# A gated linear-attention block and its MLP on one core: another sequence of turns, and the state's part of y on 128 by 64 tiles in place of 64 by 64

## The chip, the cores and the metric

The kernel runs on one core of one Trainium2 chip. The metric is the device time of one execution in microseconds (us), lower being better. Before the change the median of three executions is 481.49 us (481.31 to 482.73). The profile comes from the execution of 481.31 us; its span, from the first to the last recorded instruction, is 479.3 us.

## The reference

Two stages follow each other. The first is a gated recurrence for each of 4 batches and 8 heads, over 768 tokens with a head size of 48; the second is a LayerNorm and a two-layer MLP (384 to 1536 to 384) with a residual.

```python
def _attn_ref(q, k, v, alpha):                 # all (4, 8, 768, 48), fp32
    state = np.zeros((B, H, D, D))
    for t in range(S):
        state = alpha[:, :, t, :, None] * state + np.einsum('bhd,bhe->bhde', k[:, :, t], v[:, :, t])
        y[:, :, t] = np.einsum('bhd,bhde->bhe', q[:, :, t], state)
    return y

def _moe_ref(x, g_ln, w_ch1, w_ch2):           # x: (4, 768, 384), the heads side by side
    xn = (x - mu) / np.sqrt(var + 1e-06) * g_ln
    ch = np.maximum(xn @ w_ch1, 0.0) @ w_ch2
    return x + ch
```

The weights arrive as 64-bit floats and are rounded to fp32 on the chip.

## The kernel before

The tokens are cut into 6 chunks of 128, so there are 24 attention blocks (chunk c, batch b). One block is a Python generator with 22 steps. Each step issues a few instructions and then yields. These are the steps that matter here:

```python
    def attention(c, b):
        ...
        nc.gpsimd.tensor_mul(qk[:, 1, :, :D], raws.pop(("k", c, b)), ek)      # GpSimd: k scaled
        yield
        nc.vector.tensor_mul(qk[:, 0, :, :D], raws.pop(("q", c, b)), eq)      # VectorE: q scaled
        ...
        # TensorE: 8 transposes into qkT [112, 2, 4, 128]: head 2p in rows 0..47, head 2p+1 in rows 64..111
        for p in range(NP):                                                   # NP = 4 pairs of heads
            for i in range(2):
                rows = slice(64 * i, 64 * i + D)
                nc.tensor.matmul(aps[i][:, p], qkT[rows, 1, p], qkT[rows, 0, p], start=True, stop=True)
        yield
        for i in range(2):                                                    # VectorE: causal mask
            nc.vector.copy_predicated(out=at[:, i], data=aps[i], mask=...)
        ...
        yps = [ps.tile([P, NP, D], FP32, name=f"yps{i}", tag=("s", "a")[i], bufs=(2, 3)[i]) for i in range(2)]
        sides = [slice(64 * s, 64 * s + 64) for s in range(2)]                # the two halves of the tokens
        if c > 0:                                                             # y, part of the carried state (line 284)
            for p in range(NP):
                for i in range(2):
                    rows = slice(64 * i, 64 * i + D)
                    for s in sides:
                        nc.tensor.matmul(yps[i][s, p], qkT[rows, 0, p, s], sts[b][rows, p, i],
                                         start=(p == 0), stop=False)
        for p in range(NP):                                                   # y, part within the chunk (line 289)
            for i in range(2):
                for s in sides:
                    nc.tensor.matmul(yps[i][s, p], at[:, i, p, s], vt[:, 2 * p + i],
                                     start=(c == 0), stop=(c == 0 or p == NP - 1))
        yield
        for i in range(2):                                                    # ScalarE: y out of PSUM (line 294)
            nc.scalar.copy(out=x.rearrange("p (a b d) -> p a b d", b=2, d=D)[:, :, i], in_=yps[i])
        yield
        ...                        # sps: k'v of the chunk (line 302); st: added to the state (307), gated on GpSimd (312)
        nc.vector.bn_stats(stats, x); nc.vector.bn_aggr(mv, stats)            # LayerNorm
        ...
        nc.vector.tensor_scalar(out=xn, in0=x, scalar1=mv[:, 0:1], scalar2=rstd,   # line 323
                                op0=AOP.subtract, op1=AOP.mult)
        yield
        ...
        for f in range(NF):                                                   # TensorE: transposes of xn (line 330)
            nc.tensor.transpose(xps[:, f], xn[:, f * P:(f + 1) * P], ident)
```

`sts[b]` holds the state of a pair of heads in 112 rows and 96 columns, as two blocks of 48 by 48 on the diagonal; the rest is zero.

Other generators run beside the blocks. The MLP of chunk 0 is made of plain products (lines 342 and 354). The MLP of the later chunks uses fast matrix products of 15 and 7 multiplications (lines 515 and 409), whose sums are made ahead on GpSimd (for the weights) and on VectorE (for the activations):

```python
    def combine_first():           # sums of the first layer's weights, 17 turns of two GpSimd instructions (line 467)
        for n, op, out, x, y in (...):
            for i in range(2):
                op(out[i], x[i], y[i])         # 128x384, then 128x128
            yield
    def sums():                    # letter S
        yield from combine_first()
        yield from combine_weights()           # second layer's weights, GpSimd (line 374)
```

Every engine works through its own instructions in the order in which they were issued, and that order is set by one string. Each letter lets one generator run to its next yield:

```python
    turns = {chr(ord("a") + n): attention(n // B, n % B) for n in range(NCB * B)}       # a..x: the blocks
    turns |= {chr(ord("A") + i): take_weights(i) for i in range(len(pieces))}           # A..L: round a piece of the weights
    turns |= {"M": mlp(), "S": sums(), "R": relus(), "X": ..., "N": ...}                # X, N: sums of activations on VectorE
    with tc.manual_schedule():
        for turn in ORDER:
            next(turns[turn], None)
```

Of the kernel before, what the change touches and what calls it, by code (L numbers as in the profile page):

```python
# [9 lines left out]
FP32 = mybir.dt.float32  # L10
# [11 lines left out]


ORDER = (
    "abaacbababadacbbdaacaacadbcbbbaacdadbAbbccBbdcAbCcddbddeccfcbaBfefeahfafeagdhdfb"
    "dfcbeAaefdhcBbdedgBeedfcdecfebgicbagefcdhfCgefeigghefiahfeiggdcCdhegCEcggdcFjfAM"
    "jFegMDEjMjhhfMMffFMMMDiMegElMDhhDMhhMlFMkgiGIGihEGgHIhMHMMeMkIMIMMikMMjlGMiHHLgL"
    "JjfKMJejehMKfMJgMMKLhhKMMhMMghMhiMkiMfSSijjgSijkhglMjgXXjXkSSliSXSSMMjSlinXSkMkX"
    "XMSXjSiSXMMSkMlMSMkMSmXMSMMMMijlMMMMMXMMRlMkMMiMklMMRMmmmMiMlkRkljMnMSRnmMSjMMMM"
    "MknlMMRMMliljkmMnnMMMSRMpiMMMMmMkpmlMMkRMRoMMmMkMmRMlpoMoMNMRlNniMMNnkMSMMnNmMMm"  # L30
    "kMjMMRpMmnnlRpjolMMNkNMMMMooNMlnMMMMjlMNXjXMXnqXXMXXmXMmnXmMqpMoMMMnoMMMMmMMoqMX"
    "MoMMXqMmMMMopqorRMMopMMpMpqMmMronnoMMMMMrRMMRnsrMpMMMqpMMRppMorpmMqRqMrqMMRMoMpM"
    "tMRnMtMMMpMorMsMRrMMtMqMRsNMNtmRMMrmRMNoMoMnMqstMMMLnMMMpJrqsMMRpNnrpqMMsMNMNtMr"
    "NoqoMppMMMMMuNsXMMXXuXXXMMXsqrXvXMuMsMMMXMMMqMqXMMrqrrrtMuMMMMMtMrMMsMsuMMsMvMvR"
    "qrsMMMMRRMMusMtMtMMMuRsMMvMvMMMMtsuRMvrMMswMMMRtMuqswMMtMRsRqMMRMutMxNsttMRMvMtM"
    "NwMvRNMMNuMMurstvvMtMstRMMMxMMMMNrwNtNxMxMwMMuvMxNMMMvMtMXMXMXXvwMXvXuXXMMwuMMXw"
    "XwMMMMvMMMxMMMMMMMMMMMxXxwMMMxxuMMMMwMwxwRwMMMMMMMMxMMuxMMMMMRxRuMMxwxwMMMuMMRxR"
    "RMRMMMMRvvMuMMRNMNRwwNMuMMvMuxRxRvMMMMMNxwMMvMMxMwMNvNMvMxMwNMNwMMMMXXXXMXMXXMMX"
    "MMMXMXMMMMMMMMMMMMRMMMMMMXMMMMMRRMMMMMMMMMMMRRMMMMMRMMMMMMMMRMRMMMMMRMRMMNMMMNNM"
    "MMNMMMMMMMRMRMMMNMNMNNMMMMMMMMMM"  # L40
)


# [1 line left out]
def kernel(  # L45
# [8 lines left out]
    w_ch2: bass.AP,  # L54
    out: bass.AP,
):

# [22 lines left out]
    nc = tc.nc  # L83

    B, S, H, D = q.shape
    DM = H * D
    DF = w_ch1.shape[1]
    P = 128
    NCB = S // P
    NP = H // 2  # L90
    R = 64 + D
# [11 lines left out]
    ps = ctx.enter_context(tc.tile_pool(name="ps", bufs=2, space=bass.MemoryType.PSUM))  # L103
# [100 lines left out]
    sts = [cpool.tile([P, NP, 2, D], FP32, name=f"st{b}") for b in range(B)]  # L204
# [17 lines left out]
    def attention(c, b):  # L222
# [25 lines left out]
        qkT = work.tile([R, 2, NP, P], FP32, name="qkT", tag="qkT", bufs=2)  # L248
# [11 lines left out]
        at = ats[b % len(ats)]  # L260
        aps = [ps.tile([P, NP, P], FP32, name=f"aps{i}", tag="a", bufs=3) for i in range(2)]
# [3 lines that stand above are left out]
                nc.tensor.matmul(aps[i][:, p], qkT[rows, 1, p], qkT[rows, 0, p],  # L265
                                 start=True, stop=True)
# [7 lines left out]
                nc.sync.dma_start(gate, row.rearrange("o a c -> c (o a)"))  # L274
        yield
        vt = raws.pop(("v", c, b))
        yps = [ps.tile([P, NP, D], FP32, name=f"yps{i}", tag=("s", "a")[i], bufs=(2, 3)[i]) for i in range(2)]
        sides = [slice(64 * s, 64 * s + 64) for s in range(2)]
        if c > 0:
            for p in range(NP):  # L280
                for i in range(2):
                    rows = slice(64 * i, 64 * i + D)
                    for s in sides:
                        nc.tensor.matmul(yps[i][s, p], qkT[rows, 0, p, s], sts[b][rows, p, i],  # L284
                                         start=(p == 0), stop=False)
        for p in range(NP):
            for i in range(2):
                for s in sides:
                    nc.tensor.matmul(yps[i][s, p], at[:, i, p, s], vt[:, 2 * p + i],  # L289
                                     start=(c == 0), stop=(c == 0 or p == NP - 1))  # L290
        yield
        x_of[c, b] = x = work.tile([P, DM], FP32, name="x", tag="x", bufs=9)
        for i in range(2):
            nc.scalar.copy(out=x.rearrange("p (a b d) -> p a b d", b=2, d=D)[:, :, i],
                           in_=yps[i])
        yield
        if c + 1 < NCB:
            sps = ps.tile([R, NP, D], FP32, name="sps", tag="s")
# [294 lines left out]
    def sums():  # L593
# [4 lines left out]
        yield from combine_weights()  # L598

    turns = {chr(ord("a") + n): attention(n // B, n % B) for n in range(NCB * B)}  # L600
    turns |= {chr(ord("A") + i): take_weights(i) for i in range(len(pieces))}
    turns |= {"M": mlp(), "S": sums(), "R": relus(),
# [35 lines left out]
```

## Time and profile before

| | busy us | share of the span | instructions |
|---|---|---|---|
| TensorE matmul (PE) | 463.2 | 97% | 4032 |
| TensorE weight load (PEld) | 387.4 | 81% | 4032 |
| VectorE (DVE) | 328.5 | 69% | 571 |
| GpSimd (POOL) | 203.2 | 42% | 203 |
| ScalarE (ACT) | 152.5 | 32% | 349 |

A matmul on fp32 data is recorded as two instructions, each with its own weight load; a transpose is one. Records of matmuls overlap, because they are pipelined: the mean of 383 ns of a matmul of 256 columns is no pitch. How fast matmuls follow each other is read from the chain of waits, where 12 instructions of line 409 take 1.95 us, or from the starts of two instructions that follow each other. The span of 40 slices gives 12 us to a slice. In it the matmul engine is busy nine tenths or more of every slice but the first two, the tenth (108 to 120 us) and the last. The bytes moved are 33.9 MB, most of them in the first 84 us.

### The profile page before, as it was taken

The numbers are of one execution on the slowest core, as the hardware profiler recorded it, in microseconds if no ns is written. First come the engines' busy times: TensorE is split into PE (matmuls) and PEld (weight loads), VectorE is DVE, ScalarE is ACT, GpSimd is POOL, SyncE is SP. The second block draws the span as 40 slices with busy tenths as digits, with TensorE's granted clock in tenths as the row PEclk, the third lists the DMA queues.
The fourth block names the chain that finished last, engine by engine and source line by source line (L and its number), as shares of the span: only waits on it lengthen the run. The fifth ranks groups of instructions, "written<-read, shape, count | busy, mean of one in ns | idle before, by whom it ended". The sixth has DMA issues, their size and how long they took to land.

```text
span 479.3 us, 9886 instructions
## 1 busy us (share of the span) xinstructions
PE 463.2 (97%) x4032; PEld 387.4 (81%) x4032; DVE 328.5 (69%) x571; ACT 152.5 (32%) x349; POOL 203.2 (42%) x203
## 2 busy tenths in 40 slices
PE   5799999997999999999999999999999999999997
PEld 2668555554688899998889998889998889987996
DVE  3799899825577688748677567678565666665732
ACT  5567444501033442133351222542103152123300
POOL 5134200093479984107474217472414282145611
PEclk9999999998999999999999999999999999999999
DMA  8977466102031300232200413110010000000000
GB/s 269 335 207 218 142 197 191 42 23 60 18 84 37 98 18 12 72 101 64 72 18 0 133 51 85 34 34 1 34 36 0 2 1 18 16 34 0 2 33 34
DMA packets 32501, 33.89 MB, mean 71 GB/s; under 512 B 13108, under 2 KB 28596, under 8 KB 32456
## 3 DMA queue, kind: packets, MB, share of 16 engines
q1 hardware_dynamic: 31912, 33.12, 22.8%
q8 instruction: 32, 0.52, 0.4%
q10 hardware_dynamic: 544, 0.13, 0.1%
q14 instruction: 13, 0.11, 0.1%
HBM read 28.49 MB, written 4.76 MB: 69 GB/s over the span
## 4 chain that ended last, share of the span: by engine, by line
PE 93%; DVE 5%; ACT 1%; DMA 1%; issue 1%; DVEq 0%
PE ops L409 29%; PE hps L515 28%; PE hps L342 7%; PE ops L354 6%; PE aps L265 5%; PE yps L289 5%; PE tps L252 4%; PE lps L229 3%; PE yps L284 3%; PE sps L302 2%; PE xps L330 2%; DVE at L269 1%; DVE xn L323 1%; DMA ra<-in_alpha_dram 1%; DVE w L166 1%
## 5 line engine op out<-in xcount | busy, mean ns | idle before, releaser
L515 PE MATMUL hps<-sum,w 128*128 128x256 f32 x200 | 52.1, 383 | 0.0
L567 ACT ACTIVATE hT<-hT 128x512 f32<-128x512 f32 x60 | 36.5, 629 | 24.2 <-POOL hT L537 12.2
L409 PE MATMUL ops<-w,sum 128*128 128x192 f32 x240 | 42.6, 327 | 0.0
L409 PE MATMUL ops<-w,hT 128*128 128x192 f32 x240 | 42.5, 327 | 0.0
L409 PE MATMUL ops<-ws,hT 128*128 128x192 f32 x240 | 42.3, 326 | 0.0
L515 PEld LDWEIGHTS hps<-sum,w 128*128 128x128 f32 x200 | 36.7, 190 | 5.3
L269 DVE COPY_PREDICATED at<-consts,aps 128x512 f32<-128x512 int32 x48 | 32.1, 722 | 12.9 <-PE aps L265 12.8
L312 POOL TENSOR_TENSOR st<-st,gate 128x384 f32<-128x384 f32 x20 | 20.1, 1005 | 48.9 <-PE hps L342 23.4
L236 POOL TENSOR_TENSOR qk<-rk,ek 128x384 f32<-128x384 f32 x24 | 26.1, 1092 | 32.8 <-ACT ek L233 26.1
L409 PEld LDWEIGHTS ops<-w,sum 128*128 128x128 f32 x240 | 39.3, 190 | 0.5
L409 PEld LDWEIGHTS ops<-ws,hT 128*128 128x128 f32 x240 | 39.4, 190 | 0.3
L409 PEld LDWEIGHTS ops<-w,hT 128*128 128x128 f32 x240 | 39.2, 190 | 0.4
L427 POOL TENSOR_TENSOR ob<-u,x 128x192 f32<-128x192 f32 x10 | 7.1, 712 | 71.9 <-issue 38.5
L534 POOL TENSOR_TENSOR hT<-hT,u 128x512 f32<-128x512 f32 x10 | 13.2, 1315 | 50.3 <-DVE u L533 50.2
L354 PE MATMUL ops<-w,hT 128*128 128x384 f32 x96 | 33.5, 502 | 0.0
L342 PE MATMUL hps<-xT,w 128*128 128x512 f32 x72 | 32.4, 597 | 0.0
L252 PEld LDWEIGHTS tps<-consts,qk 128*112 128x112 f32 x192 | 22.8, 137 | 11.2 <-issue 4.0
L252 PE MATMUL tps<-consts,qk 128*112 128x128 f32 x192 | 29.8, 281 | 2.1 <-DVE at L269 1.0
L515 PE MATMUL hps<-xT,w 128*128 128x256 f32 x120 | 31.0, 381 | 0.0
L265 PEld LDWEIGHTS aps<-qkT 48*128 48x128 f32 x384 | 24.0, 187 | 7.4 <-issue 4.5
L289 PE MATMUL yps<-rv,at 128*64 128x48 f32 x768 | 27.5, 224 | 1.9 <-DVE at L269 1.4
L265 PE MATMUL aps<-qkT 48*128 48x128 f32 x384 | 28.7, 285 | 0.7 <-ACT qkT L256 0.7
(127 smaller groups left out, 939.1 us busy)
## 6 DMA issues: line engine op xcount, KB each, us to landing
ws<-in_moe_w_ch_dram SPq DMA_DIRECT2D x12, 768.0 KB
ra<-in_alpha_dram SPq DMA_DIRECT2D x24, 192.0 KB
rk<-in_k_dram SPq DMA_DIRECT2D x24, 192.0 KB
rq<-in_q_dram SPq DMA_DIRECT2D x24, 192.0 KB
rv<-in_v_dram SPq DMA_DIRECT2D x24, 192.0 KB
out_dram<-ob SPq DMA_DIRECT2D x24, 192.0 KB
row<-eq SPq DMA_DIRECT2D x20, 2.0 KB
gate<-row SPq DMA_DIRECT2D x20, 2.0 KB
```

What stands on the lines that cost most here:

```text
L229: nc.tensor.matmul(lps[:, :DM], tri, la, start=True, stop=True)
L236: nc.gpsimd.tensor_mul(qk[:, 1, :, :D], raws.pop(("k", c, b)), ek)
L252: nc.tensor.transpose(tps[:, p], qks[b][:, i, p].rearrange("p a b -> p (a b)")[:, :R], ident)
L265: nc.tensor.matmul(aps[i][:, p], qkT[rows, 1, p], qkT[rows, 0, p], start=True, stop=True)
L269: nc.vector.copy_predicated(out=at[:, i], data=aps[i], mask=mask.unsqueeze(1).broadcast_to([P, NP, P]))
L289: nc.tensor.matmul(yps[i][s, p], at[:, i, p, s], vt[:, 2 * p + i], start=(c == 0), stop=(c == 0 or p == NP - 1))
L312: nc.gpsimd.tensor_mul(st, st, gate.unsqueeze(2).broadcast_to([P, NP, 2 * D]))
L342: nc.tensor.matmul(hps, w1[:, f, j * P:(j + 1) * P], xT_of[c][:, f], start=(f == 0), stop=(f == NF - 1))
L354: nc.tensor.matmul(ops_of[b], hT_of[c][:, j, b], w2[:, j], start=(j == 0), stop=(j == NJ - 1))
L409: nc.tensor.matmul(acc, quarters(c, b)[0][n][:, j], win["b"][n][:, j], start=(j == 0), stop=(j == HJ - 1))
L515: nc.tensor.matmul(acc[:, i], w, b, start=True, stop=True)
L567: nc.scalar.activation(out=x, in_=x, func=AFT.Relu)
```

## The change

The change has two parts. In the first, the state's part of y is computed for a pair of heads at once. Before, each of the two heads had its own rows (48 of 64) and each half of the tokens its own columns, so that four tiles of 64 by 64 of the array were in use, with 48 columns of output each. Now both heads go through together: the 112 rows of `qkT` against the state's 112 rows and 96 columns, the two zero blocks included, on two tiles of 128 rows and 64 columns. That makes 8 matmuls of 96 columns for a block in place of 16 of 48. They stand between those of the chunk's own part, pair by pair. y now lies in one PSUM bank (tag `s`) instead of two (`s` and `a`), and ScalarE copies it out with one instruction instead of two.

The second part is the string. The sequence of turns is another one on all engines, [...]. Each block has the same 22 steps as before, and all other instructions and buffers are the same.

```diff
@@ the sequence of turns (16 lines; the parts that the prediction speaks of) @@
-    "abaacbababadacbbdaacaacadbcbbbaacdadbAbbccBbdcAbCcddbddeccfcbaBfefeahfafeagdhdfb"
-    "dfcbeAaefdhcBbdedgBeedfcdecfebgicbagefcdhfCgefeigghefiahfeiggdcCdhegCEcggdcFjfAM"
-    "jFegMDEjMjhhfMMffFMMMDiMegElMDhhDMhhMlFMkgiGIGihEGgHIhMHMMeMkIMIMMikMMjlGMiHHLgL"
-    "JjfKMJejehMKfMJgMMKLhhKMMhMMghMhiMkiMfSSijjgSijkhglMjgXXjXkSSliSXSSMMjSlinXSkMkX"
-    "XMSXjSiSXMMSkMlMSMkMSmXMSMMMMijlMMMMMXMMRlMkMMiMklMMRMmmmMiMlkRkljMnMSRnmMSjMMMM"
-    "MknlMMRMMliljkmMnnMMMSRMpiMMMMmMkpmlMMkRMRoMMmMkMmRMlpoMoMNMRlNniMMNnkMSMMnNmMMm"
-    "kMjMMRpMmnnlRpjolMMNkNMMMMooNMlnMMMMjlMNXjXMXnqXXMXXmXMmnXmMqpMoMMMnoMMMMmMMoqMX"
-    ... (9 lines cut)
+    "ababdaacbaabccaabacdacbaabadcbbbdcdAabbbdaBcCccdabAeddbcbdcffcdfeegacfcbagdhfbde"
+    "adbceBeegAdhfBCfdeabdfefcAheiBeafdeagjgbecfebcfcgeegfdefdgcghhihfdcgdegCCigMhMgD"
+    "DhMjEMEjFMhiDkhfMgfighFheMFFfMMIMEIhIDMgEjhMGhMgjMhgfMGiHMMGGkMMMMHeiJMkMlHJMigM"
+    "IMLJilHljMejKKjiLKeLjMhhfjSigSMhMlSMglSlhgiffMKkMhMhSSSMSSSMXiXkikXSXiimjMXXXSSM"
+    "MXkMMSkjMMXkMkMMSMMjMmMMjXkmMSlmiMSMMiMkMMXkMjMMMlMlmRMmMMMokSjlMlMnlMnMljnkMMMR"
+    "MjnMMMMSMMmMnMMmnRMMRRMoRSkiMlpklniMkpnjmMMRMmMRpkMRMNMMNmMlMiRkmMMiNMMnloMpRMSM"
+    "njNMMkplMoRMMMkMMNmjNMMlMMNNmonnMljomqMMlqMMlnXMMXMXmXnXXMXqMMMXmmXMMooMMMMpMpMn"
+    ... (9 lines cut)
@@ -274,25 +273,21 @@
                 nc.sync.dma_start(gate, row.rearrange("o a c -> c (o a)"))
         yield
         vt = raws.pop(("v", c, b))
-        yps = [ps.tile([P, NP, D], FP32, name=f"yps{i}", tag=("s", "a")[i], bufs=(2, 3)[i]) for i in range(2)]
+        yps = ps.tile([P, NP, 2, D], FP32, name="yps", tag="s")
         sides = [slice(64 * s, 64 * s + 64) for s in range(2)]
-        if c > 0:
-            for p in range(NP):
-                for i in range(2):
-                    rows = slice(64 * i, 64 * i + D)
-                    for s in sides:
-                        nc.tensor.matmul(yps[i][s, p], qkT[rows, 0, p, s], sts[b][rows, p, i],
-                                         start=(p == 0), stop=False)
         for p in range(NP):
+            if c > 0:
+                for s in sides:
+                    nc.tensor.matmul(yps[s, p].rearrange("p a b -> p (a b)"), qkT[:, 0, p, s],
+                                     sts[b][:R, p].rearrange("p a b -> p (a b)"),
+                                     start=True, stop=False)
             for i in range(2):
                 for s in sides:
-                    nc.tensor.matmul(yps[i][s, p], at[:, i, p, s], vt[:, 2 * p + i],
-                                     start=(c == 0), stop=(c == 0 or p == NP - 1))
+                    nc.tensor.matmul(yps[s, p, i], at[:, i, p, s], vt[:, 2 * p + i],
+                                     start=(c == 0), stop=(c == 0 or i == 1))
         yield
         x_of[c, b] = x = work.tile([P, DM], FP32, name="x", tag="x", bufs=9)
-        for i in range(2):
-            nc.scalar.copy(out=x.rearrange("p (a b d) -> p a b d", b=2, d=D)[:, :, i],
-                           in_=yps[i])
+        nc.scalar.copy(out=x, in_=yps.rearrange("p a b d -> p (a b d)"))
         yield
         if c + 1 < NCB:
             sps = ps.tile([R, NP, D], FP32, name="sps", tag="s")
```

The first letters S stand in the fourth line of both strings: in `MfSSijjgS` before and in `hhfjSigSMh` after. There `f`, `g` and `h` are the blocks (1, 1), (1, 2) and (1, 3).

## The prediction

> **What bounds the kernel now.** I read the shares first, then the slices, then the matmul engine's waits, then the chain of waits around the one place that stood out. The shares and slices of the page:
>
> ```profile
> PE 463.2 (97%) x4032; PEld 387.4 (81%) x4032; DVE 328.5 (69%) x571; ACT 152.5 (32%) x349; POOL 203.2 (42%) x203
> ...
> PE   5799999997999999999999999999999999999997
> ...
> PEclk9999999998999999999999999999999999999999
> ```
>
> TensorE is the bound, and it is short of work in the first two slices, in the tenth (108 to 120 us, where the granted clock also drops) and at the end. Its waits, longest first (us in total, times, longest):
>
> ```profile
> PE lps L229 <- ACT la L226: 4.3, 1, 4.3
> PE xps L330 <- DVE xn L323: 3.1, 1, 3.1
> PE yps L289 <- DVE at L269: 1.4, 2, 1.1
> ...
> PE hps L515 <- DVE hT L558: 0.8, 1, 0.8
> ```
>
> The first is the start (first data). The second is the only long wait in the steady part. The chain of waits there (start, length, what):
>
> ```profile
> 107.45 4.29 DVE xn L323
> 111.74 0.14 issue
> 111.87 0.87 PE xps L330 x3
> 112.75 3.65 PE ops L354 x8
> ...
> 124.71 0.61 PE yps L284 x32
> 125.32 1.07 PE yps L289 x32
> 126.39 2.78 PE ops L354 x8
> 129.17 0.44 PE tps L252 x4
> 129.60 2.58 PE ops L354 x8
> ```
>
> One LayerNorm subtraction takes 4.29 us. The list of the tile xn shows that this is an exception, and GpSimd's order of time shows what ran meanwhile:
>
> ```profile
> L323 DVE TENSOR_SCALAR xn<-x,mv,rstd x24: 461/476/4364, 33.9 to 407.4; 128x384 f32<-128x384 f32 x24
> ...
> 107.38 4.13 POOL L467 TENSOR_TENSOR w<-w 128x384 f32<-128x384 f32 x6
> 126.94 1.11 POOL L467 TENSOR_TENSOR rq<-w 128x384 f32<-128x384 f32 x1 [15.43 <-DVE qk L238]
> ```
>
> The median is 476 ns; this one began with a row of six GpSimd sums and ended 0.2 us after the last, when GpSimd ran out of work. When TensorE resumed, eight instructions of line 354 took 3.65 us, not the 2.58 us of a quiet place.
>
> To split the span I take from the trace the pitch of each kind of matmul instruction (start to start, same kind): 429 ns for 512 columns, 323 for 384, 216 for 256, 163 for 192, 109 for 128 (transposes); 61 for line 265, 29.2 for line 289, 28 for line 302 and 14.9 for line 284. A change of tile shape adds to this: 93 ns going into tiles (line 515 to 265: 309 for 216), 122 from line 289 or 302 and 141 from line 265 on leaving, 134 from line 284 to 289. Counts times pitches give 437.0 us, and the 121 changes of shape 14.2 us, together 451.2. The first matmul starts at 4.3 us and the end after the last start is 3.6 us. The other 20.3 us are excess: 11.5 before 48 us (waits and slow matmuls of the start), 4.8 from 108 to 120 us, 1.0 near 436 us, 3 spread out.
>
> [...] this one did not get in between six GpSimd instructions in a row, while others, at 158.1 and 187.7 us, got in between two. [...] 93 to 141 ns for a change, and 14.9 ns a step on four tiles against 29.2 on two. [...] After the 3.6 us between two matmul starts, the next ones of line 354 are 640 ns apart for some 1.5 us, not 323. A wait of 3.1 us thus cost 4.8.
>
> **The change part by part.**
>
> *State's part of y.* It removes 16 matmuls in each of the 20 blocks with c > 0, 320 in all: 640 instructions at 14.9 ns, 9.5 us. It adds 160 of 96 columns. No row has this shape, so I estimate it. Two tiles of 128 by 64 take 58.4 ns for two instructions of 48 columns; in the full array a column costs 0.835 ns ((429 − 109)/384), so 48 more columns add 40 ns. That is 98 ns for each matmul (two instructions on alternating tiles), 15.7 us in all. If the weight load came to be hidden, only 96 columns × 0.835 = 80 ns would be left, 12.8 us. So +6.1 us, at best +3.3.
>
> *Changes of shape.* State and chunk parts now share a shape, so 20 changes at 134 ns go, 2.7 us. The new sequence also has other neighbours: on TensorE I count 88 changes after for 121 before. At the costs above, 10.1 us for 14.2: −4.1 us.
>
> Sum on TensorE, which is the path: 6.1 − 4.1 = **+2.1 us** before rounding (453.3 for 451.2), −0.8 at best.
>
> *Copy of y.* Two copies of 326 ns become one of 384 columns, estimated at the 475 ns of the xT copy (same size, also from PSUM): 24 × (652 − 475) = 4 us less of ScalarE, which is 32% busy. Worth nothing directly. The tag `a` of three PSUM buffers loses one user, which may ease the start.
>
> *The sequence at 108 us.* Before, the subtraction of block (1, 3) stood on VectorE behind two sums that wait for TensorE (line 359), and so came when GpSimd was deep in its row of weight sums. After, (1, 1) and (1, 2) are placed around the first S, (1, 3) after the fourth, and the row of six S turns (`SSSMSSS`) comes behind all three. GpSimd instructions which wait for another engine (line 236) stand between S turns 2 and 3 and again after turn 4; at such places the subtractions got in before. I expect 4.8 us to shrink to 0.3. But GpSimd runs ahead freely: counting from the end of (1, 3)'s state sum, it reaches the second of these places after 0.9 + 4 × 1.45 + 1.0 = 7.7 us, and VectorE reaches (1, 3)'s subtraction after two line-354 groups, two sums and one product, 2 × 2.6 + 2 × 0.56 + 0.6 = 6.9 us. That is close. One chance in four that it misses, and then it waits some 7 us, of which I charge 6 to TensorE. Expected: −4.5 + 1.5 = **−3.0 us**.
>
> *The start.* VectorE was nearly full from 24 to 96 us before (11.6 of 12 us in most stretches), with the weight rounding. Ahead of the MLP's first product there are now 6 rounding steps of about 2.4 us on VectorE, before there were 8; the total up to the last weight piece is the same within 1 us (82.8 and 83.7). TensorE can thus start the MLP a little sooner, but the later pieces still hold it: I take **−1 us**, −3 to +2.5.
>
> Sum: 479.3 + 2.1 − 3.0 − 1.0 = 477.4 us of span. The metric is 2.2 us above the span (481.49 and 479.3): 479.6, which I round down to 479.0, because the row may also end a little faster than charged.
>
> **Rivals.** (1) *The sequence changes nothing, as VectorE's exclusion comes back elsewhere.* For it: all 24 subtractions still run beside GpSimd's work, and VectorE's sums with two SBUF inputs are stretched as well (1.1 us for 0.4 at 133 us). Against it: from 120 to 432 us all of that cost TensorE only some 2 us, since it has work queued. It would give 481 + 2 = 483.5. (2) *TensorE's work decides.* With a dearer state part, say 120 ns, the sum is +5.6 and the time about 482.5; with the cheap 80 ns it is 476. (3) *The start becomes the bound*, a weight piece arriving later than its product: the tightest place before was the fourth piece, whose rounding ended 4 us of VectorE work beyond TensorE's own; after, the tightest is 2.7 us. It speaks for a gain: 476.5. (4) *The row catches two subtractions and VectorE stands still for 12 us or more*: 487 and worse.
>
> **Range and chances.** The terms vary by about 2 (state part), 3 (the wait at 108) and 2.5 us (start), together some 4.5 us to each side: 474.5 to 484.5 us. 2% is 9.6 us, so faster would need under 471.9, all terms at their best and more, and slower over 491.1, a new stall of over 10 us. The work of all engines is the same within 1%, which leaves 0.95 for within 2%.
>
> **What would show it.** In the profile after: PE instructions 3712 (4032 − 640 + 320); the state group with about 49 ns of pitch an instruction, and with its neighbours some 1.7 to 1.75 us a block, as now (0.61 + 1.07); no subtraction on line 318 (the old 323) over 2.5 us before 130 us, and PE nines in the tenth slice with the clock at 9. If the state group shows 40 or 60 ns, the estimate of the fixed part was wrong. If a subtraction of 4 us or more stands in the chain again, the reading of GpSimd's row was wrong. If TensorE has more than 14 us of excess before 48 us, or less than 9, the start was. Wrong altogether would be a wait that the lists do not show me: for a PSUM buffer of tag `s`, which now alone holds y until it is copied out, or at the end, where the fast products of chunk 5 stand alone.

## The result, and the profile after

The changed kernel takes **475.15 us** (median; 473.87 to 475.65), the kernel before 481.71 us on the same chip (481.31 to 482.73): a ratio of 0.9857, 95% interval 0.9832 to 0.9882. The forecast of 479.0 had the direction right, and the time lies in the range (474.5 to 484.5), near its lower edge; but the gain is 6.6 us where 2.5 were forecast. The profiled span went from 479.3 to 471.8 us, by 7.5; this is what is accounted for below. It is 0.9 us more than the gain in the medians, because the profiled execution of the kernel after is its fastest, 1.3 us under its median, and that of before lies 0.4 us under its own.

The page of the kernel after, shares and slices:

```profile
PE 459.0 (97%) x3712; PEld 388.5 (82%) x3712; DVE 327.1 (69%) x571; ACT 152.0 (32%) x325; POOL 203.8 (43%) x203
...
PE   5989999999999999999999999999999999999997
...
PEclk9999999999999999999999999999999999999999
```

The 7 in the tenth slice has become a 9, and the clock is at 9 throughout. TensorE's waits (us in total, times, longest):

```profile
PE lps L228 <- ACT la L225: 5.4, 3, 4.3
PE tps L251 <- DVE at L268: 1.0, 2, 0.6
PE hps L510 <- DVE hT L553: 1.0, 1, 1.0
```

The wait for xn is gone; the first data and the end remain. The chain around the same place (start, length, what), with the first y block after it:

```profile
105.84 0.65 PE xps L325 x6
106.50 2.58 PE ops L349 x8
109.08 0.33 PE xps L325 x3
109.41 7.74 PE ops L349 x24
117.15 0.32 PE yps L281 x4
117.47 0.22 PE yps L286 x8
117.69 0.18 PE yps L281 x4
```

The chain stays on TensorE, and eight instructions of line 349 (the old 354) take the quiet 2.58 us. Lines 281 and 286 are the two parts of y. The list of xn in the kernel after (min/median/max ns), a product and the subtraction of block (1, 3) in VectorE's order of time, and GpSimd's order of time beside them:

```profile
L318 DVE TENSOR_SCALAR xn<-x,mv,rstd x24: 456/473/2862, 34.7 to 400.0; 128x384 f32<-128x384 f32 x24
...
103.78 0.98 DVE L237 TENSOR_TENSOR qk<-rq,eq 128x384 f32<-128x384 f32 x1
106.27 0.93 DVE L318 TENSOR_SCALAR xn<-x,mv,rstd 128x384 f32<-128x384 f32 x1 [1.51 <-issue]
...
100.65 1.06 POOL L307 TENSOR_TENSOR st<-st,gate 128x384 f32<-128x384 f32 x1 [27.24 <-issue]
...
105.03 0.99 POOL L235 TENSOR_TENSOR qk<-rk,ek 128x384 f32<-128x384 f32 x1
105.99 1.00 POOL L462 TENSOR_TENSOR ra<-ra,w 128x384 f32<-128x384 f32 x1
106.94 0.57 POOL L462 TENSOR_TENSOR extra<-extra,w 128x128 f32<-128x128 f32 x1
```

It waited for the sum under way (105.99 to 106.94 us) and then got in; the next sum took 0.57 us for 0.45. It was done 0.93 us after its start, not 4.36. GpSimd had no gap here: from 100.65 us on each of its instructions, those of line 235 (the old 236) included, starts before the last one's recorded end.

The span of both traces, split as the prediction split it: pitches, changes of tile shape, and excess (what lies between two starts beyond these), in us. For the new instructions of 96 columns the pitch is 45 ns, read from the chain; those of the chunk's part are counted at the 29.2 ns of before, although they follow each other at 27.5 here, so that the pitches of after are 1.1 us too high and its excess as much too low.

| | pitches | shape changes (number) | excess to 48 us | 48–100 | 100–125 | 125–415 | 415–440 | span |
|---|---|---|---|---|---|---|---|---|
| before | 436.8 | 14.2 (121) | 11.5 | 0.4 | 4.8 | 2.6 | 1.1 | 479.3 |
| after | 441.7 | 10.1 (88) | 9.8 | 0.3 | 0.1 | 0.8 | 1.25 | 471.8 |

A y block as it stands, from its first state matmul to the start of its last, takes 1584 ns after and 1528 before: +56 ns, 1.1 us for the 20 blocks. So of the 7.5 us, +1.1 is y, −1.4 are 13 other changes of shape that the new sequence saves, −4.75 is the wait at 108 us, −1.7 the start, and −0.75 the rest. The rest has a cost that the shape changes above leave out. When TensorE comes back from small tiles to the full array, the second instruction there starts late too: by about 104 ns in 51 of the 58 returns that both traces have after 48 us, and by about 50 in the others. Before has 33 such returns and after 25; their lateness adds up to 3.3 and 2.3 us.

### The profile page after: what moved, and what is told of

Same layout as the page of the kernel before. It is cut to its first block, busy times and chain, and to the rows that moved or that the text cites. A ratio compares the mean times of both kernels' runs of the same rounds, so it can differ in the third digit from the quotient of the medians.

```text
span 471.8 us, 9234 instructions
## 1 busy us (share of the span) xinstructions
PE 459.0 (97%) x3712; PEld 388.5 (82%) x3712; DVE 327.1 (69%) x571; ACT 152.0 (32%) x325; POOL 203.8 (43%) x203
## 4 chain that ended last, share of the span: by engine, by line
PE 90%; DMA 4%; DVE 2%; POOL 2%; ACT 2%; SPq 0%; issue 0%; POOLq 0%; DVEq 0%
PE ops L404 29%; PE hps L510 26%; PE hps L337 7%; PE ops L349 7%; PE aps L264 5%; PE yps L286 4%; PE yps L281 4%; PE tps L251 3%; PE lps L228 2%; PE sps L297 2%; PE xps L325 2%; DMA rk<-in_k_dram 2%; DMA ws<-in_moe_w_ch_dram 1%; DMA ra<-in_alpha_dram 1%; DVE w L163 1%; ACT ws L169 0%
## 5 line engine op out<-in xcount | busy, mean ns | idle before, releaser
L286 PE MATMUL yps<-rv,at 128*64 128x48 f32 x768 | 36.4, 219 | 0.0
L286 PEld LDWEIGHTS yps<-rv,at 128*64 128x64 f32 x768 | 33.0, 137 | 1.3 <-issue 0.7
L349 PE MATMUL ops<-w,hT 128*128 128x384 f32 x96 | 32.3, 488 | 0.0
L251 PE MATMUL tps<-consts,qk 128*112 128x128 f32 x192 | 29.2, 281 | 1.5 <-DVE at L268 1.0
```

The costliest lines, as they stand in the source:

```text
L251: nc.tensor.transpose(tps[:, p], qks[b][:, i, p].rearrange("p a b -> p (a b)")[:, :R], ident)
L286: nc.tensor.matmul(yps[s, p, i], at[:, i, p, s], vt[:, 2 * p + i], start=(c == 0), stop=(c == 0 or i == 1))
L349: nc.tensor.matmul(ops_of[b], hT_of[c][:, j, b], w2[:, j], start=(j == 0), stop=(j == NJ - 1))
```

## The experiments

### The two parts of the change, one at a time

Before's sequence with the new tiles (*tiles_only*), and the new sequence with the old tiles (*order_only*). For the second, y needs two PSUM buffers again, so that three turns in which y is copied had to move up a little.

```diff
 tiles_only: before, with
+        yps = ps.tile([P, NP, 2, D], FP32, name="yps", tag="s")     # and the matmuls and the one copy of after
 order_only: before, with after's string, and in it
-    "...dcdAabbbdaBcCcc..."  "...MMjXkmMS...XkMjMMMl..."  "...MsuMsMtu...RMMsMMRMM..."
+    "...dcdAaabbbdBcCcc..."  "...MMjjXkmMS...XkMMMMl..."  "...MsuMssMtu...RMMMMRMM..."
```

> The sequence of turns of before, with the state's part of y on 128 by 64 tiles, one bank for y and one copy. Theory (the sequence brought the gain, the tiles cost a little): the state part costs 4.9 us more on TensorE (160 matmuls at 90 ns for 640 instructions at 14.9 ns) and saves 20 changes of shape at 134 ns, so +1 to +2 us: 482.7 to 483.7 us, and the subtraction of 4.3 us at 107 us is still there. Rival (the freed PSUM bank and the single copy brought the gain): under 479 us.

> The sequence of after (three copies of y out of PSUM moved ahead in ScalarE's order, since y needs a second bank of the tag a again), with the state's part on 64 by 64 tiles and two copies. Theory: faster than both kernels, as the sequence brought 8.3 us and the tiles cost 1 to 2: 473 to 474.5 us. Rival (the sequence needs the freed bank): TensorE waits for buffers of tag a in the first 48 us or later, and the time is over 477 us.

*tiles_only* took 482.83 us, beside 482.1 for before: 1.002 (1.0007 to 1.0033). Its list of waits keeps the wait for xn:

```profile
PE xps L325 <- DVE xn L318: 3.2, 1, 3.2
```

The tiles alone cost about 1 us and take no wait away. *order_only* took 477.41 us: 0.9905 (0.9879 to 0.9932), 4.7 us faster, not the whole gain; its rival came true. Its wait at 108 us is gone (excess 0.2), but it has others that after does not have, at 234 us (the first line) and at 33 us (the second):

```profile
PE lps L229 <- ACT qkT L256: 1.2, 1, 1.2
...
PE lps L229 <- ACT eq L234: 0.7, 1, 0.7
```

Its excess between 125 and 415 us is some 4 us, where after has 0.8. The sequence and the tiles are thus not two independent parts. To see which side of the tiles matters, after's kernel was run with the three moved turns alone (*after_moved*), and then with y in two banks and two copies besides, the 128 by 64 tiles being kept (*two_banks*):

```diff
 two_banks: after_moved, with
-        yps = ps.tile([P, NP, 2, D], FP32, name="yps", tag="s")
+        yps = [ps.tile([P, 2, 2, D], FP32, name=f"yps{i}", tag=("s", "a")[i], bufs=(2, 3)[i]) for i in range(2)]
-        nc.scalar.copy(out=x, in_=yps.rearrange("p a b d -> p (a b d)"))
+        for i in range(2):
+            nc.scalar.copy(out=x[:, i * 192:(i + 1) * 192], in_=yps[i].rearrange("p a b d -> p (a b d)"))
```

> After, with nothing but the three copies of y that order_only has ahead in ScalarE's order. Theory (the moves are harmless, and order_only lost its 4 us to the tiles and banks): within 0.5 us of after, 0.985 to 0.987 of before. Rival (the moves cost it): 0.988 to 0.992, like order_only, with the wait of 1.2 us of line 228 at about 230 us.

> The kernel after_moved, with y in two banks again (two pairs of heads in tag s, two in tag a, two copies of 192 columns), but on 128 by 64 tiles. Theory (the bank and the second copy are what the new sequence can't afford): the waits of order_only come back, with 2 us more of excess in the first 48 us and the wait at about 230 us: 0.989 to 0.992. Rival (the tiles' shape and its changes of mode are it): as after_moved, 0.985 to 0.987.

*after_moved* took 474.48 us, 0.9842 (0.9804 to 0.9880); the moves cost nothing that shows. *two_banks* took 477.01 us, 0.9889 (0.9852 to 0.9925), in line with *order_only*. Its excess between 125 and 415 us is 2.8 us against *after_moved*'s 1.1, and the wait of line 228 (old 229) for qkT is back, at 233 us:

```profile
PE lps L228 <- ACT qkT L255: 1.2, 1, 1.2
```

The 2 us expected in the first 48 us did not come (10.8 us of excess, 11.4 in *after_moved*). So the second bank and the second copy together cost some 2.5 us under this sequence, of which the excess shows 1.7; which of the two does it was not tried. The shape of the tiles, with its better and worse matmuls, makes little difference beside that (477.41 and 477.01 us): its worth is that y fits into one bank and one copy.

### Is it that one subtraction?

In *before*, the times of two kinds of VectorE instruction spread: the subtraction, a `tensor_scalar` (461 to 4364 ns, median 476), and the product of two tiles in SBUF (line 238, 526 to 1384 ns, median 548). Those of `bn_stats` (527 to 560 ns) and of the masked copy (702 to 752 ns) do not. Writing the subtraction's output as three pieces of 128 columns in rows of 129 keeps the work; that it would then no longer wait for GpSimd was the author's guess. In *before_1port* all 24 subtractions are so written, in *one_1port* only that of block (1, 3).

```diff
-        xn = work.tile([P, DM], FP32, name="xn", tag="xn", bufs=2)
-        nc.vector.tensor_scalar(out=xn, in0=x, ...)
+        xn = work.tile([P, NF, P + 1], FP32, name="xn", tag="xn", bufs=2)
+        nc.vector.tensor_scalar(out=xn[:, :, :P], in0=x.rearrange("p (f c) -> p f c", c=P), ...)
```

> Before, with the LayerNorm subtraction written into rows of 129 elements instead of 128, so that its source (384 in a row) and its destination (3 rows) no longer have the same form. Theory [...]: the operation [...] is slower by itself (550 to 600 ns for 476) but waits for GpSimd nowhere, so the wait at 107 us is gone and with it 4.8 us: 476 to 478 us. Rival 1 (any VectorE operation that reads SBUF is held by that row, or the wait was for something else): it stays at 4 us, 481 to 482.5. Rival 2 [...]: 476 ns as before and the long wait too.

> Before, [...] the one that waited 4.3 us at 107 us; all others as in before. Theory: that one instruction is worth the whole 4.8 us (3.3 us of waiting and 1.5 us of slow matmuls), and nothing else changes: 0.988 to 0.992 of before, about 477 us, and the excess of the first 48 us stays at 11.5. Rival (the next subtraction or another VectorE operation falls into the row in its place): a new wait of TensorE before 125 us, and over 0.995.

*before_1port* took 478.53 us, 0.9934 (0.9919 to 0.9949), 0.5 us over what was expected. Its list of xn, and a wait that before does not have:

```profile
L323 DVE TENSOR_SCALAR xn<-x,mv,rstd x24: 641/666/673, 34.9 to 405.2; 128x384 f32<-128x384 f32 x24
...
PE xps L330 <- DVE st L307: 1.3, 2, 1.1
```

No subtraction waits any more, and the excess from 100 to 125 us falls from 4.8 to 0.15; but each takes 666 ns for 476, and the excess up to 100 us grows by 2.7 us. *one_1port* took 476.82 us, 0.9883 (0.9844 to 0.9921). The subtraction in VectorE's order of time, with GpSimd's row and the chain on TensorE beside it:

```profile
107.95 0.65 DVE L328 TENSOR_SCALAR xn<-x,mv,rstd 128x384 f32<-128x384 f32 x1
...
108.00 4.14 POOL L472 TENSOR_TENSOR w<-w 128x384 f32<-128x384 f32 x6
...
109.34 0.33 PE xps L335 x3
109.66 2.58 PE ops L359 x8
```

The same six sums run, the subtraction takes 0.65 us beside them, and TensorE does not wait there: 4.8 us of excess becomes 0.15. By the times it is 5.4 us faster than before (482.24 us beside it). One instruction of 571 on VectorE carried the largest part of what the change gains, without any new sequence.

### Why that one waited through six sums

In the kernel after, the subtraction waited for the end of one sum and took 0.93 us in all; in *before* it waited for six and took 4.36 us. The first idea was that a row of sums which depend on nothing else shuts VectorE out.

Three kernels were to put the subtraction into after's own row of six sums. In *after_xn_late* its turn stands later in the string; in *xn_in_row* and *xn_in_row2* VectorE also runs 6 and 10 `bn_stats` ahead of it, whose result is not used.

```diff
-    "...MlSMglSlhgiffMKkMhMhSSSMSSSMX..."
+    "...MlSMglSlgiffMKkMMkhhhSSSMSSSMX..."        # in all three
+        if (c, b) == (1, 3):
+            for _ in range(10):                      # 6 in xn_in_row
+                nc.vector.bn_stats(idle, x)
```

> After, with the subtraction of block (1, 3) behind two mask copies, a sum and the product of q of block (2, 2) on VectorE, and its transposes behind one more projection on TensorE, so that it is issued at about 110 us, in the middle of GpSimd's row of ten sums without a wait for another engine (109.8 to 117 us). Theory (such a row is never let go between its instructions): the subtraction takes 5 us or more and ends with the row, TensorE waits 3 to 5 us for it and then runs slowly: 478 to 482 us. Rival (it gets in after the one or two GpSimd instructions that run, and the case at 107 us in before was another cause): under 1.6 us, and within 1.5 us of after, 474 to 476.5.

> The kernel after_xn_late, with six BatchNorm statistics into a scratch tile ahead of block (1, 3)'s subtraction, since that was issued at 107.3 us, too early for the row: now at about 110.6 us, with the ten sums from 110.1 to 117 us that wait for each other. Theory A (such a row never lets it in): the subtraction takes 5 us or more, and TensorE waits 4 us or more for it, 478 us and more. Theory B (it gets in after the running sum): under 1.6 us, TensorE waits under 1 us, 474 to 476.5 us.

> The kernel xn_in_row with ten statistics for six, so that the subtraction comes at about 113.2 us, within the six weight sums in w1 itself (the same six as at 107.4 us in before). Theory C: under 1.6 us, as everywhere else. Theory A (these six, which read and write w1, keep it out): 3 us or more, to their end. TensorE waits for it in both cases, as it comes 2 us later than its transposes: 1.5 to 3 us in C, over 5 in A.

*after_xn_late* (474.16 us, 0.9851, 0.9795 to 0.9908) and *xn_in_row* (474.19 us, one execution) missed the row: the subtraction came at 107.3 and 110.8 us, ahead of the six sums, and took 608 and 462 ns. They decide nothing. *xn_in_row2* (478.85 us, one execution) hit it, at 113.44 us:

```profile
113.44 0.80 DVE L322 TENSOR_SCALAR xn<-x,mv,rstd 128x384 f32<-128x384 f32 x1
...
113.03 2.48 POOL L466 TENSOR_TENSOR w<-w 128x384 f32<-128x384 f32 x3
```

Among the same six sums it got in after one, in 798 ns. (The kernel is slower only because the transposes waited 2.4 us for this late subtraction.) So the six sums do not shut VectorE out by themselves, and the first idea falls.

A second idea was the exact moment of arrival. Two kernels shift before's subtraction by a `bn_stats` of 180 or 384 columns ahead of it.

```diff
+        if (c, b) == (1, 3):
+            nc.vector.bn_stats(idle, x[:, :180])     # shift_330; shift_600 has 384
```

> Before, with one BatchNorm statistic of 180 columns into a scratch tile ahead of block (1, 3)'s subtraction, so that it comes about 0.33 us later, in the middle of the running weight sum of 384 columns and not as one takes over from another. Theory C (the moment of arrival decided): it gets in after that sum, under 1.3 us, TensorE's wait at 108 us is gone, about 477 us. Theory A (the kind of row keeps it out, whenever it comes): 3.5 to 4.2 us, to the end of the row at 111.5 us, about 482 us.

> The same with a statistic of 384 columns, 0.6 us later. Theory C: under 1.3 us and about 477 us. Theory A: 3.2 to 3.8 us and about 482 us.

*shift_330* (481.83 us, one execution) in VectorE's and GpSimd's order of time:

```profile
107.94 4.13 DVE L326 TENSOR_SCALAR xn<-x,mv,rstd 128x384 f32<-128x384 f32 x1
...
107.72 4.13 POOL L470 TENSOR_TENSOR w<-w 128x384 f32<-128x384 f32 x6
```

At 107.94 and, in *shift_600* (482.25 us, one execution), at 108.46 us it took 4132 and 3932 ns: to the end of the row each time, whatever the moment.

What is left is measured by kernels that compute nothing of the reference: a row of GpSimd sums in SBUF, VectorE busy with `bn_stats` (0.55 us each beside the sums in *rows_long*, as in *before*), then one subtraction of the same shape.

```python
s = ...                                         # ScalarE starts row and VectorE together
for i in range(n):
    add(o[0], o[0], o[2]); add(o[1][:, :128], o[1][:, :128], o[3][:, :128])    # GpSimd's row
for _ in range(delay):
    nc.vector.bn_stats(st, s)
nc.vector.tensor_scalar(out=y, in0=s, scalar1=..., scalar2=..., op0=AOP.subtract, op1=AOP.mult)
```

The first two have short rows, of 8 sums (12 where sizes alternate). *rows_alone* varies how the sums depend on each other, *rows_phase* the moment of arrival in 32 steps of some 10 ns.

> GpSimd's rows by themselves: nothing of the computation is done. Sixteen stages; in each, GpSimd runs a row of 8 sums of 384 columns (or 6 pairs of 384 and 128), and VectorE, after one, two or three BatchNorm statistics, runs one tensor_scalar of 384 columns with two pointer scalars (or, in the fourth stage of each kind, a sum of two SBUF tensors). The kinds: all sums from the same sources (apart); each from the one before (chain); the same in place (inplace); pairs in place, as in the weight sums. Theory A (a row in which each sum needs the one before never lets VectorE in): the tensor_scalar takes under 1.6 us in apart, and 5 us or more, to the row's end, in chain and inplace. Theory B (it gets in after the running instruction in all of them, and the wait of 4.3 us at 107 us had another reason): under 1.6 us everywhere. Theory C (chance of the phase decides): both kinds of duration within one kind of row, depending on the number of statistics ahead.

> GpSimd's row of pairs by itself (384 and 128 columns in turn, in place, no gap between them), 32 stages; nothing of the computation is done. VectorE's tensor_scalar arrives some 10 ns later from stage to stage: in the first 16 from 70 ns before to 70 ns after a sum of 384 columns takes over from one of 128, in the last 16 the same where one of 128 takes over from one of 384. In before, the subtraction of 4.36 us started 60 ns before the end of the running sum of 128 columns and 18 ns before the start record of the next. Theory C (the moment of arrival decides: [...]): in one or a few neighbouring stages the tensor_scalar takes over 3 us, to the end of the row, in all others under 1.6 us. Theory B (it always gets in after the sum that runs or has just begun): under 1.6 us in all 32, and what held the subtraction at 107 us stays open.

No subtraction was shut out: 591 to 1315 ns in *rows_alone*, and in *rows_phase*, in the list of the output tile:

```profile
L67 DVE TENSOR_SCALAR y<-s,col x32: 464/947/1282, 6.5 to 274.2; 128x384 f32<-128x384 f32 x32
```

Here a subtraction that came 128 ns or less before the end of a sum lost to the next sum as well, one that came 137 ns or more before it did not. The limit is not sharp: one that came 145 ns before it in *rows_alone* and one at 179 ns in a later kernel (*rows_pairs*) lost too. That is one sum more, and no explanation of six. In the trace before, though, the six sums were only the end of something. GpSimd's order of time in the kernel before, from its last gap on:

```profile
96.49 0.82 POOL L312 TENSOR_TENSOR st<-st,gate 128x384 f32<-128x384 f32 x1 [12.20 <-issue]
97.27 0.99 POOL L236 TENSOR_TENSOR qk<-rk,ek 128x384 f32<-128x384 f32 x1
...
106.01 1.00 POOL L467 TENSOR_TENSOR rk<-rk,w 128x384 f32<-128x384 f32 x1
106.97 0.45 POOL L467 TENSOR_TENSOR extra<-extra,w 128x128 f32<-128x128 f32 x1
```

It had run since 96.49 us without a gap, and the subtraction came at 107.36 us, in its fifteenth instruction (twelve sums and three products). In between there was no turn of VectorE, by which is meant from here on an instruction of one of the two kinds whose times spread: a `tensor_scalar`, or one with two inputs in SBUF. *rows_long* therefore has rows of 26 sums, and arrivals 1 to 12 us into them.

> GpSimd's rows of 26 sums by themselves (384 and 128 columns in turn, in place, both sources and the destination in one tile, as the six weight sums), 14 stages; nothing of the computation is done. VectorE's tensor_scalar arrives after 2, 5, 8, 11, 14, 17 or 20 BatchNorm statistics, 1 to 12 us into the row; in the last seven stages GpSimd's row is followed by a sum that waits for VectorE's result, as the row of before was. Theory D (a row that has run for long [...] does not let it in any more): from some stage on the tensor_scalar takes 3 us or more, to the row's end. Theory E (the row in front of a wait for VectorE stays closed): the last seven take long, the first seven under 1.6 us. Theory B: under 1.6 us in all, and what closed the row of before stays open.

The long wait came back. Arrivals up to 8.2 us into the row got in within 0.6 to 1.2 us; at 11.8 us they waited 6205 and 6209 ns, to the end of the row; at 10.0 us one waited (7989 ns) and one got in (778 ns). A wait for VectorE behind the row (theory E) does not decide it: both halves have short waits up to 8.2 us and the long one at 11.8 us. Two more kernels tell age, number and gaps apart. In each of its last two rows *rows_kinds* has two subtractions, which tells the age of the row from the time since VectorE's last turn. Its rows of one size turned out to leave 78 ns between sums, as each sum needs the one before. *rows_pairs* has two alternating chains in those too, so that each sum starts 40 ns before the end of the last.

```diff
 rows_pairs, rows of one size w = 128 or 384
-            add(o[0][:, :w], o[0][:, :w], o[2][:, :w])
+            add(o[0][:, :w], o[0][:, :w], o[2][:, :w]); add(o[1][:, :w], o[1][:, :w], o[3][:, :w])
```

> Nothing of the reference is computed. In the run before this one, a subtraction that came 8.2 us or less into a row of GpSimd sums got in after one or two of them, and one that came 11.8 us into it waited 6.2 us, to the row's end; at 10.0 us it went once each way. Here 16 rows of about 20 us: five of 384 and 128 columns in turn, with the subtraction 8.9, 9.5, 10.1, 10.7 and 11.3 us into the row; five of 128 columns (0.41 us each) with 7.1, 8.3, 9.5, 10.7 and 11.9 us; four of 384 columns (0.95 us each) with 8.3, 9.5, 10.7 and 11.9 us. Theory of age (the row closes [...]): in all three kinds the subtractions at 10.7 us and later wait to the row's end, 7 to 10 us, and those at 9.5 us and earlier get in within 1.3 us. Theory of number (it closes after about 15 sums): in the rows of 128 columns all five wait, for 8 to 12 us, as 16 sums and more have gone by; in the rows of 384 columns none waits, as 12 have gone by at most. In the last two rows VectorE subtracts twice, after 4.8 and again 7.6 us later (12.4 us into the row), and after 7.1 and again 5.3 us later. [...] if it is the row's own age, the second ones wait to its end, some 7 us.

> Nothing of the reference is computed. The run before this one had, in its rows of one size, each sum waiting for the one before it, with 78 ns between them, and there the subtraction always got in; in the rows of two sizes, where two chains of sums alternate and each sum starts 40 ns before the end of the last, it got in at 8.8 and 9.4 us and waited to the row's end at 10.0, 10.6 and 11.2 us. Here the rows of one size have two chains too: eight rows of sums of 128 columns (0.41 us each) with the subtraction 4.8, 6.0, 7.1, 8.3, 9.5, 10.1, 10.7 and 11.9 us into the row, and eight of 384 columns (0.95 us each) with 8.3, 8.9, 9.5, 10.1, 10.7, 11.3, 11.9 and 13.1 us. Theory of age (a row without a gap closes at about 10 us): in both kinds the subtractions at 10.1 us and later wait to the row's end (some 6 to 10 us), the earlier ones get in within 1.3 us. Theory of number (it closes after 14 to 15 sums): of 128 columns those at 7.1 us and later wait, of 384 columns none does, as at most 13 sums have gone by. If none waits in either, it takes sums of two sizes, and neither age nor number alone closes a row.

Four arrivals of *rows_pairs* in VectorE's order of time (start, us):

```profile
31.95 0.63 DVE L60 TENSOR_SCALAR y<-s,col 128x384 f32<-128x384 f32 x1
54.14 13.79 DVE L60 TENSOR_SCALAR y<-s,col 128x384 f32<-128x384 f32 x1
...
306.06 0.88 DVE L60 TENSOR_SCALAR y<-s,col 128x384 f32<-128x384 f32 x1
...
326.20 6.52 DVE L60 TENSOR_SCALAR y<-s,col 128x384 f32<-128x384 f32 x1
```

The first two are in rows of 128 columns: 5.8 us into the row, in the fifteenth sum, it got in; 7.0 us into it, in the eighteenth, it waited 13.8 us. The other two are in rows of 384 columns: 11.8 us into the row but in its thirteenth sum it got in; the last came in a row that followed the one before without a gap, some 20 sums after VectorE's previous turn, and waited 6.5 us.

| counted from GpSimd's last gap, or from VectorE's last turn if that is later | sums of two sizes | of 128 columns | of 384 columns |
|---|---|---|---|
| up to 14 sums | all got in (up to 9.4 us) | in at 12 sums | in at 9, 10, 12, 13 sums (up to 11.8 us) |
| 15 sums | *before*, *tiles_only*, *rows_kinds* shut out; *rows_long* once each way | in (5.8 us) | |
| 16 and more | all shut out (from 10.6 us) | all shut out (at 18 sums and more, from 7.0 us) | all four at 19 or 20 sums shut out |
| rows with 78 ns between sums | | all got in, up to 49 sums | all got in, up to 12 sums |

So it is the number of sums, not the age: the age theory falls in both directions (in at 11.8 us, out at 7.0). And it counts from VectorE's last turn: in *rows_kinds* a second subtraction, in the eighteenth sum of its row but eleven sums after the first one, took 465 ns, and in *rows_alone*, where the first four rows left no gap, subtractions in the sixteenth and the thirty-first sum got in, each some seven sums after VectorE's last turn. This also fits *xn_in_row2*, whose row had run for 16 sums, but in which a product of VectorE with two inputs in SBUF had got in nine sums earlier. And it tells why after's row is harmless: at 106.27 us it was at its seventh instruction, and VectorE's product at 103.78 us had got in three before. What in the hardware counts the sums is not shown; rows of other operations were not tried, and each of these kernels ran once.

### The place that was left: the end

After's last wait, 1.0 us of line 510 for hT of line 553, is at 429 us, where GpSimd adds two pairs for the same product. The one that TensorE's buffer waits for stood second. *after_swap* exchanges them:

```diff
             sub(u2, u2, acc)
-            add_late(c1, c1, u2)
             add_late(c5, c5, u2)
+            add_late(c1, c1, u2)
```

> After, with the two GpSimd sums that use the eighth product's difference exchanged, so that the last third of the hidden layer (c5) is ready 1.3 us sooner for the last VectorE subtraction of a round. In the last chunk, where nothing else is left to do, TensorE waits 1.0 us for that subtraction (at 428 us) and runs slowly or late for a little more, 1.25 us in all. Theory: that goes away: 0.5 to 1.2 us less than after, 0.983 to 0.9845 of before. Rival (another sum or a ReLU then comes late in its place, as c1 is ready later): no difference, 0.9855 to 0.987.

It took 473.46 us (472.95 to 473.89), 0.9818 (0.9781 to 0.9855). The wait is gone from the list:

```profile
PE lps L228 <- ACT la L225: 5.5, 3, 4.2
PE tps L251 <- DVE at L268: 0.9, 2, 0.5
PE aps L264 <- DVE at L268: 0.8, 1, 0.8
```

and the excess from 415 to 440 us goes from 1.25 to 0. It is faster than before by 1.5 to 2.2%. Against after's sequence the trace shows the 1.25 us. *after_moved*, beside it, has an interval that overlaps (0.9842, 0.9804 to 0.9880), though each execution of *after_swap* was faster than each of *after_moved* (474.31 to 475.84).

## Why the prediction was right, and where it was off

The direction came true, the size did not, and two steps failed. The larger is a cost: TensorE's own work was to grow by 2.1 us and fell by 0.3, because the instructions of y cost less than estimated. The other is the wait at 108 us, put at −3.0 us and measured at −4.75: the subtraction was thought to get in only where GpSimd waits for another engine, and to risk 7 us otherwise; it got in between two sums of a row without a gap.

*What bounds the kernel.* Right: TensorE before and after, and the wait at 108 us as the one place worth much. *one_1port* shows that the one subtraction was worth the 4.7 us read from the excess. With no wait the tenth slice shows no lower clock (from 108 to 120 us the granted clock was 0.86 in *before* and is 1.00 in the kernel after), and all 4.8 us are gone, not just the 3.1 of the wait. (The slow stretch was somewhat longer than read: three steps of line 354 took 639 to 641 ns, 1.9 us, not 1.5.) The signs that it named came: 3712 instructions, a 9 in the tenth slice, 9.8 us of excess to 48 us, and no subtraction over 2.5 us before 130 us.

*State's part of y.* The sign was right, the size wrong. The prediction took 49 ns an instruction; the chain shows 45 (0.18 us for four), and the chunk's part between them costs 27.5 ns an instruction (0.22 us for eight) where 29.2 were assumed. The first makes 1.3 us, the second 1.1. So y costs +1.1 us, where the prediction's 6.1 − 2.7 says +3.5. The prediction contradicted itself here: its sign to look for, 1.7 to 1.75 us a block, is what came (0.32 + 3 × 0.18 + 4 × 0.22 = 1.74), but its own sum would have made it 1.85. The changes of shape were as counted, 33 fewer. TensorE in all: −0.3 us, not +2.1.

*Copy of y.* The copy takes 479 ns, 475 were estimated. ScalarE's total fell by only 0.5 us, not 4: the two copies of a block overlap, so that all 48 kept it busy for 12.7 us, not 48 × 326 ns, and the 24 new ones for 11.5; the prediction had taken a mean duration for a pitch. "May ease the start" was wrong: the freed bank and the saved copy are worth 2.5 us together, most of it between 125 and 415 us, and only with the new sequence. The prediction took the string and the tiles as two terms to be added. *tiles_only*, *order_only* and *two_banks* show that they aren't: the old string gains nothing from the free bank, and the new one loses without it.

*The sequence at 108 us.* That GpSimd's row held the subtraction, and that the new place would free it, was right; how it gets in was not. The prediction counted on the places where line 236 waits for another engine, and charged 1.5 us for one chance in four that (1, 3) would miss the last of them and be shut out by the row behind it. In the kernel after, line 235 waits at neither of these places (it starts at 105.03 and 108.86 us, in a row that has run since 100.65 us). The subtraction came among sums and got in. *xn_in_row2* shows it getting in even among the six, and the long rows show why: what shuts it out is a row of some 15 or more sums since VectorE's last turn, not the six that the list had grouped in one line. Reading the row from its last line alone was the mistake: in before it starts at 96.49 us. Measured −4.75 us for −3.0.

*The start.* −1.7 for −1.0. The MLP's first product does start sooner, at 46.3 us for 49.1. How much of it is the change stays unsettled: the kernels with both parts of the change have 9.8 to 11.4 us of excess there, the others 11.5 to 12.9, and part of that is the clock. In the profile of *after_moved*, the one with 11.4 us, the granted clock is down to 8 tenths in the third slice (24 to 36 us), where after has 1.00; over its four executions the mean clock went from 0.996 to 1.000.

```profile
PEclk9989999999999999999999999999999999999999
```

*Elsewhere.* The prediction gave nothing; it was −0.75 us, and the eight fewer returns to the full array account for 1.0 us less. Its cost of a change of shape left out the late second instruction. By these terms the span forecast of 477.4 was 5.6 us too high: 2.4 on TensorE, 1.75 at 108 us, 0.7 at the start, 0.75 elsewhere. They all lie on the same side, so the small terms did not cancel as the range had assumed.

*Rivals.* (1) The exclusion is still there: a subtraction of 2862 ns at 158.5 us, behind a single long GpSimd sum, while TensorE has work. Before has one like it, 2774 ns at 178.0 us. Neither costs anything seen. (2) and (3) were both in part right: the cheaper state part and the start each gave a gain. (4) did not happen.

## What to carry to other kernels

Where an instruction is stretched by another engine, look at the whole row of that other engine back to its last gap, not at the line beside it, and price the one instruction by giving it a form in which it does not wait: here one output layout was worth 4.7 us. A sequence belongs to the buffers it runs with: the part of the change that frees a bank and saves a copy was worth nothing with the old sequence and 2.5 us with the new one, so run both halves. When a sum of terms and a sign to look for come from the same estimate, work out one from the other before putting either down.

## What the runs showed of the hardware

- In these runs GpSimd's sums of 128 and 384 columns in SBUF let a waiting `tensor_scalar` of VectorE in at one of the next two ends of a sum (0.46 to 1.35 us in all), unless about 15 of them had followed each other without a gap since VectorE's last turn. From 16 on it waited until the row ended: 3.9 to 13.8 us. Gaps of 78 ns between sums of 128 columns kept the row open for up to 49 sums; for 384 columns only 12 were tried.
- In *rows_phase* a subtraction that arrived 128 ns or less before the end of a sum lost to the next one too (678 to 754 ns in all with a next sum of 128 columns, 1211 to 1282 with one of 384).
- The subtraction of 384 columns takes 641 to 673 ns with an output in three pieces (*before_1port*, *one_1port*) and did not wait once in 25 cases, and 456 to 481 ns in one piece (*before* and the kernel after), when it doesn't wait.
- A matmul instruction of 96 columns on a 128 by 64 tile has a pitch of 45 ns, where one of 48 columns has 27.5 to 29.2.
- After a return from small tiles to the full array the second instruction starts late as well, by about 104 ns in 51 of 58 returns (after 48 us, in the two kernels).
